# Conversion's shift through two PSUM banks, and a list scheduler with one time for the shared ports

## The chip, the cores and the metric

The kernel runs on one core of a Trainium2 chip. A core has engines that run their own queues of instructions in order: TensorE (PE) for matmuls, whose weight loads are shown apart as PEld; VectorE (DVE); ScalarE (ACT); GpSimd (POOL); and SyncE (SP), which here only issues DMAs. SBUF is the large on-chip memory, PSUM the small one of eight banks into which PE writes its results; DVE and ACT read and write both.

The metric is the device time in microseconds (us) of one execution; lower is better. The kernel before takes 739.78 us, the median of three runs (738.67 to 739.96).

## The reference

Two blocks follow one another. In the first, every one of 8 batches and 8 heads has 512 tokens and 32 state rows of width 64, and each side attends to the other. In the second, the 4352 rows that come out (8 batches of 512 + 32 rows, 512 wide) go through a hidden layer of 2048 with the gate h * cos(h).

```python
    scores = scale * np.matmul(x, state.transpose(0, 1, 3, 2))
    ...
    xread = np.matmul(a, state)
    ...
    sread = np.matmul(a2, x)
    return np.concatenate([xread, sread], axis=2).astype(np.float32)
    ...
    h = x @ w_in
    g = h * np.cos(h)
    return (g @ w_out).astype(np.float32)
```

`x` and `state` are float32. The weights `w_in` (512 x 2048) and `w_out` (2048 x 512) arrive as float64, so the kernel makes float32 of them itself.

## The kernel before

**Stages.** The batches are taken in four pairs. For a token row the attention output is a weighted mix of the 32 state rows of its head, so the kernel multiplies the state by `w_in` first ("products", `per_head`, L312, copied out at L462) and then multiplies the attention weights by that result (`hidden`, L488). What `hidden` makes for 128 hidden columns of one batch is called a tile; a batch has 16, the first pair 32 (steps 0 to 31, `FIRST = 32`). A tile passes through the gate: ACT rounds h to an integer (`gate`, L564), DVE takes the difference (`gate2`, L567), ACT the sine (`gate3`, L570), DVE the product with h (`gate4`, L584), which goes to `g_all`. In the first pair, `hidden` writes to two single PSUM banks in turn, so a tile's matmuls wait until `gate4` of the tile two before has read its bank. Output products with `w_out` are L640 for the first pair's first batch, and a seven-product form (L772) for everything after, for which sums of quarters of the weights (`inner`, L689; `sums_of`, L1325) are formed and kept in DRAM (`blocks_kept`).

**Conversion.** `fetch` (L210) brings a piece of float64 weights to SBUF as pairs of 32-bit words. `convert` makes float32 of it in five steps: "1" on ACT (L223) takes the absolute high word as a float with a changed exponent; "2" on ACT (L226) takes the top bits of the low word; "b" on DVE (L229) shifts the result of "1" left by 3, in place; "c" on DVE (L232) puts in the sign from the high word; "d" on POOL (L237) adds what "2" made. There are 18 pieces: 0 to 3 have 512 columns, 4 to 17 have 1024.

**The side banks.** Two PSUM banks, `h_pairs[1]` with the halves `side_banks`, are used in the first pair for the products L312 and for one set of state transposes (L161). The planner calls their halves `sd00`, `sd01`, `sd10`, `sd11`. The two remaining pairs of banks are `at` (attention) and `acc` (output products).

**The order.** Up to the end of the first pair, and a little into the next, the order of instructions comes from a list scheduler that runs while the program is built. `first_pair_tasks` lists tasks with an engine, an estimated cost, the names of what they read and write, a due step and a mark `shares`[...]. `link` turns due steps to times (22 + PACE * step) and finds what each task must wait for. `first_pair` takes, engine by engine, the task that can start soonest, and among those within NEAR of it the one due first; a task marked `shares` is put behind POOL's task of that time (`pool_busy`). Where PE would idle early on, dummy matmuls (`warm`, L952) are put in. The estimates only decide the order; on the chip every engine follows its queue, and semaphores hold it where a result is missing. After the first pair a hand-written plan sets the order (`later_pair`, `plan`, `stages`), which the change doesn't touch.

Of the kernel before, what the change touches and what calls it, by code (L numbers as in the profile page):

```python
# [11 lines left out]
I32 = mybir.dt.int32  # L12
# [10 lines left out]
def kernel(  # L23
# [189 lines left out]
    def convert(i, p):  # L213
# [7 lines left out]
        e = e.bitcast(I32)  # L221
        if p == "1":
            nc.scalar.activation(dst, raw.bitcast(F32)[:, :, :, 1],  # L223
                                 func=ACTF.Abs, scale=2.0 ** -112)
        elif p == "2":
            nc.scalar.activation(e, raw.bitcast(U32)[:, :, :, 0],  # L226
                                 func=ACTF.Copy, scale=2.0 ** -29)
        elif p == "b":
            nc.vector.tensor_scalar(bits, bits, 3, None,  # L229
                                    op0=ALU.logical_shift_left)  # L230
        elif p == "c":
            nc.vector.scalar_tensor_tensor(out=bits, in0=raw[:, :, :, 1],  # L232
                                           scalar=-2 ** 31, in1=bits,
                                           op0=ALU.bitwise_and,
                                           op1=ALU.bitwise_xor)
        else:
            nc.gpsimd.tensor_tensor(bits, bits, e, op=ALU.add)  # L237
# [10 lines left out]
    class Attention:  # L248
# [207 lines left out]
        def products_kept(self, nt, bank=None, c0=0, c1=WC, copy=None,  # L456
                          js=(0, 1)):
            to = at if bank is None else side_banks
            if c0 == 0:
                sw_of[self.b, nt] = sw_all[:, nt % 2]  # L460
# [257 lines left out]
    class Product:  # L718
# [4 lines left out]
        def __init__(self, name, pr, row):  # L723
# [5 lines left out]
            products.append(self)  # L729
            self.first = len(stage_list)  # L730
# [392 lines left out]
    def first_pair_tasks():  # L1123
# [35 lines left out]
        def conversion(i, due):  # L1159
            n = 512 if i < 4 else 1024  # L1160
            raw, w, e = raw_of(i), weight_of(i), low_of(i)
            if i > (6 if f64 else 4):
                add("sp", .4, lambda: fetch(i), "", raw, due - 3)
            for p, engine, cost, r, wr, sh in (
                    ("1", "act", act(n) + .05, raw, w, False),
                    ("2", "act", act(n) + .05, raw, e, False),
                    ("b", "dve", n * .0007 + .03, w, w, True),
                    ("c", "dve", dve(n), raw + " " + w, w, True),
# [4 lines left out]
        def attention(b, k):  # L1173
# [30 lines left out]
            m2 = k + 6 if b == 0 else k + 5  # L1204
            if b == 0:
# [3 lines left out]
                add("dve", .46, a.inverse1, "m10 m11", "m10 m11", k + 5)  # L1209
# [9 lines left out]
            if b == 0:  # L1219
# [4 lines left out]
                add("dve", .3, a.inverse2, "i20 i21", "i20 i21", m2 + 2)  # L1224
            else:
                add("act", 5.0, a.exps, "at0 at1 m20 m21",
                    f"z{z}0 z{z}1 xT2 xT3 i20 i21 m20 m21", m2)
                for j in range(2):
# [3 lines left out]
                    "m10 m11 i20 i21", k + 7)  # L1232
# [54 lines left out]
        def tile_(t, k):  # L1287
# [11 lines left out]
                k + 2)  # L1299
# [97 lines left out]
        def p5_tasks(k):  # L1397
# [3 lines left out]
            for i, (r, w) in enumerate(((lo, q1), (hi + " " + q1, q1),  # L1401
                                        (lo + " " + hi, q3)), 1):
                add("pool", 4 * pool(512), lambda i=i: pd.sums(i), r, w,
# [3 lines left out]
            for i in range(5):  # L1407
# [12 lines left out]
                elif i == 2:  # L1420
                    add("dve", .36, follow, "acc0 sums1", "sums2", at_)
                    add("pool", 4 * pool(512), lambda: pd.sums(4),
# [6 lines left out]
        def p3_sums(k):  # L1429
            pd = products_[1]  # L1430
            add("pool", 4 * pool(512), lambda: pd.sums(1),
# [17 lines left out]
        for step, what in (  # L1449
                (1, lambda: attention_late(0, 1)),  # L1450
                (3, lambda: products(0, 1, 3)),
                (3, lambda: add("pe", .4, lambda: states(1, side_banks[0]),
                                "held0", "sd00 sd01", 6)),
                (3, lambda: add("act", .53,
                                lambda: states_kept(1, side_banks[0]),
                                "sd00 sd01", "stT1", 6)),
                (5, lambda: attention(1, 5.0)),
                (7, lambda: products(0, 2, 7)),
                (11, lambda: products(0, 3, 11)),
                (13, lambda: products(1, 0, 15)),  # L1460
                (13, lambda: attention_late(1, 14)),
                (13, lambda: inner(0, a11, 5, temps[0], names(TEMPS), 15)),
                (15, lambda: sends(2, a22, 8, 17)),
                (15, lambda: sums_of(SQ, A21, A22, add_, 16, "pool")),
                (16, lambda: products(1, 1, 19)),
                (16, lambda: inner(3, matrix(SQ), SQ, temps[1], E, 15)),
                (17, lambda: sums_of(A22, SQ, A11, sub_, 18, "pool")),
                (17, lambda: attention(2, 18)),
                (18, lambda: sums_of(A21, A11, A21, sub_, 19, "dve")),
                (20, lambda: products(1, 2, 23)),  # L1470
                (20, lambda: inner(5, matrix(A21), A21, temps[0],
                                   names(TEMPS), 20)),
                (20, lambda: sends(1, a12, 6, 22)),
                (21, lambda: inner(4, matrix(A22), A22, temps[1], E, 21)),
                (23, lambda: sums_of(SQ, A12, A22, sub_, 24, "dve")),
                (24, lambda: inner(6, matrix(SQ), SQ, temps[0], names(TEMPS),
                                   25)),
                (24, lambda: products(1, 3, 27)),
                (25, lambda: attention_late(2, 23.0)),
# [4 lines left out]
        for step, what in (  # L1484
                (26, lambda: outer(0, 2, 0, 0, 26, "dve")),
                (27, lambda: outer(0, 2, 0, 1, 27, "dve")),
                (28, lambda: tokens_of_next(30)),
                (28, lambda: products(2, 0, 28)),
                (28, lambda: p5_tasks(29.5)),
                (29, lambda: weight_columns(t32, 30)),  # L1490
                (29, lambda: add("dve", .7, lambda: halves(2, 0), "z00 z01",
                                 "E0", 30)),
                (29, lambda: add("dve", .7, lambda: halves(2, 1),
                                 "z00 z01 E0", "E1", 30)),
# [5 lines left out]
        for step, t in enumerate(all_tiles[0:FIRST]):  # L1500
# [3 lines left out]
            if 4 <= step < 4 + NH:  # L1504
                first(step - 4, step + 1)
            for i in range(NH):
                if SECOND_AT[i] == step:
                    second(i, step + 2)
# [6 lines left out]
    CONV_DUE = (3, 4.5, 3.5, 6, 7.5, 7, 9, 9.5, 10.5, 11, 12, 14.5, 14, 15)  # L1515
    PACE, NEAR, SEND = 3.8, 0.3, 2.5
# [37 lines left out]
    def first_pair():  # L1554
# [20 lines left out]
        pool_busy, cold = (0.0, 0.0), True  # L1575
        log = []
        while can:
            best = None
            for e in free:
# [4 lines left out]
                for t in mine:  # L1584
                    at_ = max(free[e], ready[t])
                    if t.shares and pool_busy[0] <= at_ < pool_busy[1]:
                        at_ = pool_busy[1]
                    starts[t] = at_
# [3 lines left out]
                if best is None or starts[t] < best[0]:  # L1592
                    best = starts[t], t
            at_, t = best
# [11 lines left out]
            if t.engine == "pool":  # L1606
                pool_busy = at_, end
# [139 lines left out]
```

## Time and profile before

| what | value |
|---|---|
| median of 3 runs | 739.78 us (738.67 to 739.96) |
| the profiled execution | 740.65 us, of which the span from first to last instruction is 738.9 |
| PE busy | 708.2 us, 96% of the span |
| DVE, ACT, POOL busy | 506.8, 347.3, 542.5 us |
| mean granted PE clock | 0.993 of full speed |
| DMA | 111.33 MB, mean 151 GB/s |

The busy shares in 40 slices of 18.5 us each (a digit is a tenth, 9 is 90% or more) show that the first six slices, about the first pair, differ from the rest:

```profile
PE   8898889999999999999999999999999999999997
DVE  4989979957866668849756577768665467355550
ACT  5799675654463446343634464344634533211110
POOL 1557789375998997588998665879989665799600
```

PE has digits of 8 only there, while DVE and ACT are at their fullest. In the page's groups of instructions, a row gives line, engine, operation, output and input, count, busy time and mean duration; a group's mean mixes free and delayed executions, so single ones are read from the timeline.

### The profile page before, as it was taken

The page shows a single profiled execution, that of the slowest core. Times are in us where ns is not written, and L with a number is a line of the kernel's source. Part 1 is how long each engine was busy: PE and PEld are TensorE (multiplying, and loading weights), DVE is VectorE, ACT ScalarE, POOL GpSimd, SP SyncE. Part 2 cuts the span into 40 slices and gives each one's busy share as a digit, 9 for nine tenths or more (in the row PEclk, how much of TensorE's full clock was granted, in tenths as well). Part 3 has the DMA queues.
Part 4 walks back from the last instruction along what each step waited for, and adds up shares of the span by engine and source line. Part 5 has one row for each costly group of instructions (what it writes and reads, how often), then busy time and mean ns, then how long its engine had stood idle before and what let it go on. Part 6 is the DMA issues. An engine that isn't in the chain of part 4 may idle for free.

```text
span 738.9 us, 10734 instructions
## 1 busy us (share of the span) xinstructions
PE 708.2 (96%) x3626; PEld 519.0 (70%) x3626; DVE 506.8 (69%) x703; ACT 347.3 (47%) x586; POOL 542.5 (73%) x524
## 2 busy tenths in 40 slices
PE   8898889999999999999999999999999999999997
PEld 3343343477778878777778788777688788888886
DVE  4989979957866668849756577768665467355550
ACT  5799675654463446343634464344634533211110
POOL 1557789375998997588998665879989665799600
PEclk9999999999999999999999999999999999999999
DMA  9966799536346964693238635762225466456662
GB/s 297 285 192 193 236 265 301 122 96 150 87 128 117 214 172 115 142 197 86 82 80 168 160 96 116 147 154 83 75 68 119 115 205 143 108 156 203 155 152 46
DMA packets 204021, 111.33 MB, mean 151 GB/s; under 512 B 149888, under 2 KB 166784, under 8 KB 203968
## 3 DMA queue, kind: packets, MB, share of 16 engines
q1 hardware_dynamic: 202880, 110.14, 57.4%
q8 instruction: 29, 0.48, 0.3%
q10 hardware_dynamic: 960, 0.39, 0.2%
q14 instruction: 24, 0.20, 0.1%
q0 software_dynamic: 128, 0.13, 0.1%
HBM read 87.03 MB, written 23.59 MB: 150 GB/s over the span
## 4 chain that ended last, share of the span: by engine, by line
PE 59%; POOL 21%; DVE 9%; issue 3%; DMA 3%; ACT 2%; SPq 1%; ACTq 0%; POOLq 0%; DVEq 0%
PE o L772 29%; POOL g_all L715 16%; PE h L543 13%; PE h L488 8%; POOL swS_all L521 3%; PE at L312 3%; PE at L877 2%; DMA held<-in_state_dram 2%; PE o L640 2%; POOL sw_all L521 2%; DVE g_all L715 1%; PE at L417 1%; DVE q_all L567 1%; DVE g_all L232 1%; DVE g_all L584 1%
## 5 line engine op out<-in xcount | busy, mean ns | idle before, releaser
L715 POOL TENSOR_TENSOR g_all<-g_all 128x512 f32<-128x512 f32 x252 | 332.5, 1349 | 61.8 <-DVE g_all L715 40.4
L772 PE MATMUL o<-g_all 128*128 128x256 f32 x1456 | 343.7, 381 | 2.4 <-POOL g_all L715 2.4
L772 PEld LDWEIGHTS o<-g_all 128*128 128x128 f32 x1456 | 273.7, 190 | 49.7 <-issue 5.7
L567 DVE TENSOR_TENSOR q_all<-q_all,h 128x1024 f32<-128x1024 int32 (+1 forms) x88 | 85.3, 971 | 40.7 <-ACT q_all L564 40.4
L564 ACT ACTIVATE q_all<-h 128x1024 int32<-128x1024 f32 (+1 forms) x88 | 73.1, 833 | 81.2 <-PE h L543 35.1
L584 DVE TENSOR_TENSOR g_all<-h,q_all 128x1024 f32<-128x1024 f32 (+1 forms) x88 | 85.7, 973 | 24.5 <-ACT q_all L570 23.6
L570 ACT ACTIVATE q_all<-q_all,halfpi 128x1024 f32<-128x1024 f32 (+1 forms) x88 | 84.2, 957 | 38.7 <-DVE q_all L567 38.5
L551 DVE TENSOR_TENSOR h<-h,sums_all 128x256 f32<-128x256 f32 x96 | 41.3, 430 | 77.5 <-PE h L543 60.2
L488 PE MATMUL h<-aT_all,sw_all 128*128 128x512 f32 x128 | 64.0, 628 | 13.0 <-DVE g_all L584 12.3
L543 PE MATMUL h<-aT_all,sw_all 128*128 128x256 f32 x192 | 59.6, 392 | 3.8 <-DVE g_all L584 3.4
L543 PE MATMUL h<-aS_all,swS_all 128*128 128x256 f32 x192 | 60.2, 395 | 2.6 <-ACT sums_all L529 1.8
L715 DVE TENSOR_TENSOR g_all<-g_all 128x1024 f32<-128x1024 f32 x42 | 62.0, 1490 | 0.1
L543 PE MATMUL h<-aS_all,sw_all 128*128 128x256 f32 x192 | 58.0, 384 | 0.1
L488 PEld LDWEIGHTS h<-aT_all,sw_all 128*128 128x128 f32 x128 | 23.2, 195 | 44.3 <-issue 21.5
L521 POOL TENSOR_TENSOR swS_all<-sw_all 128x128 f32<-128x128 f32 x48 | 22.5, 468 | 41.8 <-ACT sw_all L462 41.8
L543 PEld LDWEIGHTS h<-aS_all,swS_all 128*128 128x128 f32 x192 | 33.9, 189 | 27.0 <-issue 12.1
L780 ACT COPY o<-o 128x256 f32<-128x256 f32 x26 | 9.3, 357 | 85.1 <-PE o L772 85.1
L543 PEld LDWEIGHTS h<-aT_all,sw_all 128*128 128x128 f32 x192 | 34.5, 189 | 16.3 <-DVE g_all L584 12.2
L237 POOL TENSOR_TENSOR w_in<-w_in,aS_all 128x1024 int32<-128x1024 int32 (+1 forms) x10 | 22.3, 2241 | 29.9 <-DVE w_in L232 27.2
L787 ACT COPY o<-sums_all 128x256 f32<-128x256 f32 x26 | 9.8, 378 | 68.2 <-PE o L772 68.2
L543 PEld LDWEIGHTS h<-aS_all,sw_all 128*128 128x128 f32 x192 | 35.6, 190 | 8.2 <-DVE h L551 2.7
L607 DVE SCALAR_TENSOR_TENSOR held<-o,held 128x512 f32<-128x512 f32 x38 | 25.9, 681 | 13.7 <-PE o L772 13.1
(116 smaller groups left out, 931.6 us busy)
## 6 DMA issues: line engine op xcount, KB each, us to landing
g_all<-blocks_kept SPq DMA_DIRECT2D x206, 256.0 KB, 2.8
blocks_kept<-g_all SPq DMA_DIRECT2D x48, 256.0 KB, 3.9
g_all<-in_moe_w_out_dram SPq DMA_DIRECT2D x8, 1024.0 KB, 5.7
out_dram<-ot SPq DMA_DIRECT2D x128, 64.0 KB, 2.0
g_all<-in_moe_w_in_dram SPq DMA_DIRECT2D x6, 1024.0 KB, 7.1
x_b<-in_x_dram SPq DMA_DIRECT2D x24, 256.0 KB, 4.7
xT<-in_x_dram SPq DMA_DIRECT2D x80, 64.0 KB, 2.8
x_b<-in_x_dram SPq DMA_DIRECT2D x16, 128.0 KB, 4.3
```

Of the source, the lines that this page charges most:

```text
L237: nc.gpsimd.tensor_tensor(bits, bits, e, op=ALU.add)
L488: nc.tensor.matmul(out=t.hp, lhsT=t.lhs(i), rhs=t.rhs(i), start=(i == 0), stop=(i == t.kn - 1))
L521: nc.gpsimd.tensor_tensor(o, x1, x2, op=op)
L543: nc.tensor.matmul(out=out_, lhsT=w, rhs=r, start=start, stop=True, skip_group_check=True)
L551: nc.vector.tensor_tensor(o, h2[:, LO], sums_all[:, 0], op=ALU.add)
L564: nc.scalar.activation(t.q.bitcast(I32), t.hp, func=ACTF.Copy, bias=0.25)
L567: nc.vector.tensor_tensor(t.q, t.q.bitcast(I32), t.hp, op=ALU.subtract)
L570: nc.scalar.activation(t.q, t.q, func=ACTF.Sin, bias=halfpi, scale=-TWO_PI)
L584: nc.vector.tensor_tensor(g, t.hp, t.q, op=ALU.mult)
L607: nc.vector.scalar_tensor_tensor(out=out.t[:, ch], in0=bank, scalar=TWO_PI, in1=b.t[:, ch], op0=ALU.mult, op1=ALU.add)
L715: engine.tensor_tensor(o[:, i:i + n], x1[:, i:i + n], x2[:, i:i + n], op=ALU.subtract)
L772: nc.tensor.matmul(out=o, lhsT=ring[(self.first + k) % NB][:, i], rhs=g[:, i], start=(start and i == 0), stop=(i == QT - 1), skip_group_ch ...
```

## The change

Four things are changed, all of them before the end of the first pair.

- In `convert`, step "b" of the pieces of 1024 columns (4 to 17) writes its shifted words to the two side banks in PSUM (`shifted`), and step "c" reads them there and writes the weights' tile as before. Pieces 0 to 3 stay in SBUF.
- The planner's tasks follow: for those pieces "b" and "c" are no longer marked `shares`, "b" has the cost of a DVE operation at the normal rate, and both name the side banks. Some small DVE tasks (the inverses, `halves`) are newly marked `shares`, and the cost of POOL's sums for the seven-product form is halved in the plan.
- The scheduler keeps one time, `lock`[...]; POOL's tasks wait for it too, and of tasks with the same start the one that asked first goes first.
- Nearly all due steps, and PACE and NEAR, have new values. `products_kept` sets up its entry of `sw_of` at whichever half comes first, so the halves of the first columns can come in either order.

```diff
@@ convert
+        shifted = bits if i < 4 else h_pairs[1].bitcast(I32)
...
         elif p == "b":
-            nc.vector.tensor_scalar(bits, bits, 3, None,
+            nc.vector.tensor_scalar(shifted, bits, 3, None,
                                     op0=ALU.logical_shift_left)
         elif p == "c":
             nc.vector.scalar_tensor_tensor(out=bits, in0=raw[:, :, :, 1],
-                                           scalar=-2 ** 31, in1=bits,
+                                           scalar=-2 ** 31, in1=shifted,
@@ products_kept
-            if c0 == 0:
+            if (self.b, nt) not in sw_of:
@@ conversion
+            x, narrow = (w, True) if i < 4 else ("sd00 sd01 sd10 sd11", False)
+            b_cost = n * .0007 + .03 if narrow else dve(n)
...
-                    ("b", "dve", n * .0007 + .03, w, w, True),
-                    ("c", "dve", dve(n), raw + " " + w, w, True),
+                    ("b", "dve", b_cost, w, x, narrow),
+                    ("c", "dve", dve(n), raw + " " + x, w, narrow),
@@ attention
-                add("dve", .46, a.inverse1, "m10 m11", "m10 m11", k + 5)
+                add("dve", .46, a.inverse1, "m10 m11", "m10 m11", k + 5,
+                    True)
@@ first_pair_tasks, some of the due steps
-                (7, lambda: products(0, 2, 7)),
-                (11, lambda: products(0, 3, 11)),
-                (13, lambda: products(1, 0, 15)),
+                (7, lambda: products(0, 2, 8.5)),
+                (11, lambda: products(0, 3, 19.5)),
+                (13, lambda: products(1, 0, 21.5)),
...
-                (17, lambda: attention(2, 18)),
+                (17, lambda: attention(2, 23.5)),
...
-                first(step - 4, step + 1)
+                first(step - 4, step - 0.5)
...
-                    second(i, step + 2)
+                    second(i, step + 10.0)
...
-    CONV_DUE = (3, 4.5, 3.5, 6, 7.5, 7, 9, 9.5, 10.5, 11, 12, 14.5, 14, 15)
-    PACE, NEAR, SEND = 3.8, 0.3, 2.5
+    CONV_DUE = (1.9, 1.9, 3.0, 5.1, 5.3, 5.4, 9.4, 10.5, 10.6, 11.7, 12.2, 13.3, 13.0, 15.2)
+    PACE, NEAR, SEND = 3.6, 0.1, 2.5
@@ first_pair
-                    at_ = max(free[e], ready[t])
-                    if t.shares and pool_busy[0] <= at_ < pool_busy[1]:
-                        at_ = pool_busy[1]
-                    starts[t] = at_
+                    asked = max(free[e], ready[t])
+                    shares = t.shares or e == "pool"
+                    starts[t] = max(asked, lock) if shares else asked
...
-                if best is None or starts[t] < best[0]:
-                    best = starts[t], t
+                asked = max(free[e], ready[t])
+                if best is None or (starts[t], asked) < best[0:2]:
+                    best = starts[t], asked, t
...
-            if t.engine == "pool":
-                pool_busy = at_, end
+            if t.shares or t.engine == "pool":
+                lock = end
```

## The prediction

> **What bounds the kernel now.** I first cut the span into stretches. Columns: stretch and length, then the busy time of PE, PEld, DVE, ACT and POOL with instruction counts, the granted clock, the DMA share, GB/s.
>
> ```profile
> core 0: us, PE busy (x) PEld busy (x) DVE busy (x) ACT busy (x) POOL busy (x), PEclk, DMA share, GB/s
> 20.00:36.00 16.00, 13.23 (x90) 6.35 (x91) 15.79 (x28) 12.36 (x20) 7.12 (x5) 1.00 0.92 279
> 36.00:100.50 64.50, 54.75 (x246) 22.81 (x245) 59.31 (x69) 55.49 (x84) 45.91 (x22) 0.95 0.73 210
> 100.50:145.00 44.50, 42.57 (x188) 19.75 (x187) 39.34 (x50) 28.00 (x54) 35.87 (x24) 1.00 0.79 236
> 145.00:172.00 27.00, 27.00 (x126) 17.81 (x126) 14.77 (x21) 13.74 (x26) 16.16 (x20) 1.00 0.45 103
> 172.00:738.90 566.90, 554.12 (x2925) 444.62 (x2923) 367.99 (x520) 227.80 (x392) 432.43 (x444) 1.00 0.53 130
> ```
>
> From 145 us on PE is the bound, and no edit reaches past the first pair of batches, which ends near 172. What can change lies between 20 and 145: there PE is idle 2.77 + 9.75 + 1.93 = 14.4 us, while DVE is busy 59.3 of 64.5 us in the long stretch. The waits of PE up to 185 us (engine, line and what it waited for; us in total, times, longest) name the cause:
>
> ```profile
> PE h L488 <- DVE g_all L584: 12.3, 9, 3.5
> PE h L488 <- DVE aT_all L393: 0.7, 1, 0.7
> ```
>
> A tile's matmuls wait for a bank that the last gate step (L584) of the tile two before frees, and that step is late in DVE's queue. Why DVE is late shows in its timeline (start, duration, line, operation):
>
> ```profile
> 70.84 2.03 DVE L373 TENSOR_SCALAR i_all<-i_all 128x34 f32<-128x34 f32 x1
> 74.33 0.69 DVE L229 TENSOR_SCALAR g_all<-g_all 128x1024 int32<-128x1024 int32 x1
> 75.05 1.23 DVE L232 SCALAR_TENSOR_TENSOR g_all<-g_all 128x1024 int32<-128x1024 int32 x1
> 80.31 1.76 DVE L229 TENSOR_SCALAR g_all<-g_all 128x1024 int32<-128x1024 int32 x1
> 83.19 3.40 DVE L232 SCALAR_TENSOR_TENSOR g_all<-g_all 128x1024 int32<-128x1024 int32 x1
> 83.17 2.34 POOL L237 TENSOR_TENSOR g_all<-g_all,aS_all 128x1024 int32<-128x1024 int32 x1
> 166.07 1.22 DVE L567 TENSOR_TENSOR q_all<-q_all,h 128x1024 f32<-128x1024 int32 x1 [1.05 <-ACT q_all L564]
> ```
>
> The same shift takes 0.69 or 1.76, the same combination 1.23 or 3.40; the long one began with POOL's L237. That is a lock between DVE and POOL. Finally PE's clock after a pause (timeline, then a stretch as above):
>
> ```profile
> 82.73 2.90 PE L488 MATMUL h<-aT_all,sw_all 128*128 128x512 f32 x4 [2.02 <-DVE g_all L584]
> 97.27 3.68 PE L488 MATMUL h<-aT_all,sw_all 128*128 128x512 f32 x4 [3.48 <-DVE g_all L584]
> 97.20:99.00 1.80, 1.73 (x2) 0.84 (x3) 1.80 (x3) 1.77 (x4) 1.72 (x2) 0.53 1.21 255
> ```
>
> **The change, part by part.** Part 1, the shift writes PSUM and the combination reads it there: the 14 conversions of 1024 columns (the four of 512 stay). Lock time that goes, as duration less the free one (0.69 a shift, 1.28 a pair, 1.22 a combination): shifts at 60.18 0.46, 64.71 1.60, 80.31 1.07, 92.12 1.07, 98.64 1.06; combinations at 83.19 2.18 and 100.43 0.95. Sum 8.4 us. What it costs: no row has a shift into PSUM. Lower end 0.60 (today's pace: two take 1.28 to 1.29); upper end 1.22, the L567 row of 1024 columns with a PSUM operand, whose pace, start to start, is 1.14. I take 1.14, since one PSUM operand is what the new shift has: 14 x (1.14 - 0.60) = 7.6 us. [...]the move alone hardly relieves DVE. It relieves POOL, which the same lock held: L1325 79.20 x2 took 4.00 for 2 x 1.27, 89.50 x2 3.83, L237 63.22 x2 6.03 for 2 x 2.36, and so on, about 8 us by the same subtraction. POOL bounds nothing before 145 (45.9 of 64.5), so I cost that at nothing; its cover is that slack.
>
> The combination stays at 1.14 (pace of L232 today). [...]The trace's L567 rows, one PSUM operand, agree: 0.67 to 0.71 throughout, also under POOL's work.
>
> A wait is added: both side banks now carry shifts, the weight products (L312) and the second state transposes. Behind a waiting shift queue the gate steps. Bounds: 0, or one product and its two copies, 1.02 + 1.07 us, for each of some four meetings, 8 us. In the new order each shift after a product has two or more DVE operations or attention's eight between; I take 0.
>
> Part 2, the new order, read from the order of the instructions in the changed program. The edits to costs, due steps, PACE, NEAR, the lock's time and the test on sw_of issue nothing themselves; they act through this order alone. (The weight sums L1325 stand at L1331 there, the other lines one or two further.) (a) Start. The second half of the first weight columns is converted first; all four shifts, four combinations, the two maxima and the two copies stand ahead of L373 and L393. Against today, where L393 ends at 23.8, there come 2 x 0.34 + 2 x 0.6 + 2 x 0.6 + 0.7 = 3.8 us before it, and POOL's d steps (4 x 1.27, from 18.6, each locking out a combination) reach to about 25. So the first tile starts near 28 instead of 23.35. Then, before the first L584: shift and combination three times (6.8), two gate steps, two state reads; first L584 at 37.3 for 33.5 today. One conversion more is then done. The third tile's L567 comes at about 40.6 (39.9 at best, 41.2 if PE runs at the lower clock after its pause around 24): 3.1 us later than 37.48.
> (b) From there to the L567 of the 17th tile, today 37.48 to 103.13 = 65.65 us. Today: 28 gate steps x 0.60 = 16.8; 12 shifts 7.2; 12 combinations x 1.13 = 13.6; attention 14 x 0.61 + 0.85 = 9.4; two L1325 2.3; sum 49.3. Lock: 8.4, L373 1.5, L393 1.0, L1325 0.8 = 11.7. Bracketed waits for ACT 3.5. Remainder 1.1. New: 16.8 + 11 shifts 12.5 + 11 combinations 12.5 + 9.4 + one L1325 1.1 = 52.3; lock only on L373, L393, L1325, which the planner now knows: 2.0 (ends 0 and 3); waits 3.5 + 1.0, because ACT has 13 us of work between the gates of the fifth and sixth tile (two table loads at 1.28 among it) and L584 of the sixth waits for it; remainder 1.1. Sum 59.9: 5.7 us less. With (a): 5.7 - 3.1 = 2.6 us earlier.
> (c) From the 17th tile on PE has the work. It is 0.8 us less (one second product, 1.72, done before; one L312 group, 1.02, and 0.1 later). The half clock at 97.27 goes if the 3.5 us pause goes: 3.68 - 1.84 = 1.8. Of the pauses after 100.5 (0.42, 1.16, 0.34) the 1.16 should go, since four second products (6.9 us) now stand beside the third attention: 0.9 net. One further warm-up matmul pair at the start fills a pause.
> (d) DMAs: the same transfers in another order. Two weight loads instead of one stand ahead of the eight x loads on SP's queue; [...]x then lands near 42, and its last use is near 46. Nothing on the path.
>
> Sum: 2.6 + 0.8 + 1.8 + 0.9 = **6.1 us less**. The profiled execution has 740.65 (span 738.9 and 1.75 around), so 734.55; it lies 0.87 above the median of the runs, which gives **733.7**.
>
> [...]here 2.02 us, shortly after pauses of 2.07 and 0.97, was enough for 0.74 and 0.58. [...]by the trace any 2 us pause can cost 1 to 2. The one I expect at the sixth tile (some 3 us) may so take back 1.8: in the range.
>
> **The rivals.**
> 1. *The start and the slow shifts win: slower.* For: the 7.6 us are sure and the first tile is 5 us late; the lock can move to L373, L393 and L1325, which stay. If (b) saves nothing, DVE is 3.1 us late; one more pause at half clock is 1.8; less 0.8 of work done: 4.1 us slower, 743.9. Decides from: L567 of the 17th tile after 105. Against: two thirds of the lock was on the operations moved.
> 2. *The combination still contends* (one of its inputs stays in SBUF): 2.18 + 0.95 stay, 736.8. Against: the L567 rows.
> 3. *Side banks:* one product's 2.1 us stalls twice: 733.7 + 4.2 = 737.9. For: a shift waits for PE and ACT together. Against: the distance in DVE's queue, above.
> 4. *PE stays fed:* ACT waits and lock both go (4.5 + 2.0), start only 2.4 late: 6 us more, 727.7. For: PE's idle time and slow clock (14.4, and about 3.5 of stretched tiles) allow it. Against: ACT is busy 55.5 of 64.5 us as well.
>
> **How the numbers follow.** Forecast, 730.5 to 736: 0.48. Rival 4, 724 to 730.5: 0.16. Rivals 2 and 3, 736 to 738.3: 0.18. Within 0.2% (738.3 to 741.3), about what can be told from no change: 0.08. Rival 1: 0.10. Faster 0.82. The range 727.5 to 739.0 leaves out rival 1, half of no change and the far end of 4, together just under 0.2; the forecast's own is 730.5 to 736.
>
> **What would show it.** L229 of 1024 columns into h near 1.2 each and never 1.7; its L232 never above 1.3; L237 at 2.34 to 2.4; first L488 near 28; L567 of the 17th tile near 100; no 3.68 us tile there; after it PE without pauses; after the first pair the same rows, earlier by one constant. A first L488 past 30, or the 17th tile past 105, would make it wrong; so would shifts at 0.7, to the other side.

## The result, and the profile after

The changed kernel takes 735.45 us in the median of five runs (733.81 to 736.73), the kernel before 739.78 (738.62 to 740.00). The ratio is 0.9944, 95% interval 0.9926 to 0.9962: 4.3 us faster. The profiled execution has 736.73 us, its span 734.9, where the kernel before had 740.65 and 738.9. The same kernel was run once more among the experiments (E12): 0.9943 (0.9923 to 0.9963), profiled at 735.53 with a span of 733.6.

In the changed file the lines stand one or two further: shift L230, combination L233, GpSimd's last step L238, `hidden` L489, gate L565, L568, L571, L585, output products L641 and L774, products L313 with their copies L463, first softmax L374 to L394, second softmax L357 and L362 with its transposes L401, weight sums L1331.

First the busy shares of the changed kernel in 40 slices of the span, from its page:

```profile
PE   8798899999999999999999999999999999999997
DVE  4889979868767567849756687768665367355551
ACT  4699975644544455443634373444634533211110
POOL 1557599557998896579989665879989665799600
```

PE falls from 8 to 7 in its second slice (18 to 37 us, the start), and rises from 8 to 9 in its sixth, the end of the long stretch. The same kernel in stretches (columns as in the prediction):

```profile
20.00:36.00 16.00, 11.08 (x55) 4.84 (x56) 14.09 (x20) 10.46 (x17) 7.04 (x5) 0.68 0.71 245
36.00:100.50 64.50, 59.82 (x288) 26.49 (x292) 59.52 (x78) 59.53 (x91) 42.70 (x24) 1.00 0.78 225
100.50:145.00 44.50, 44.50 (x216) 19.77 (x201) 37.27 (x51) 29.68 (x56) 34.32 (x29) 1.00 0.82 233
145.00:172.00 27.00, 26.47 (x121) 19.63 (x121) 16.74 (x24) 12.78 (x23) 14.39 (x15) 1.00 0.54 128
```

TensorE is idle 4.92 + 4.68 + 0 = 9.6 us between 20 and 145, 14.4 before. In the long stretch it gained 5.1 us of work although VectorE is as full as it was (59.5). The price stands in the first row: 2.2 us more idle time and a granted clock of 0.68. The waits of PE up to 185 us (us in total, times, longest):

```profile
PE h L489 <- DVE g_all L585: 4.3, 3, 2.6
PE at L401 <- ACT xT L362: 4.2, 1, 4.2
PE h L489 <- ACT sw_all L463: 0.5, 1, 0.5
```

The wait for the gate's last step fell from 12.3 to 4.3 us, and a new one of 4.24 us stands at the start. VectorE's timeline shows why the gate comes sooner, with one line of GpSimd's between:

```profile
31.07 1.22 DVE L233 SCALAR_TENSOR_TENSOR w_in<-g_all,h 128x1024 int32<-128x1024 int32 x1
32.33 1.23 DVE L230 TENSOR_SCALAR h<-w_in 128x1024 int32<-128x1024 int32 x1
33.59 1.22 DVE L233 SCALAR_TENSOR_TENSOR w_in<-g_all,h 128x1024 int32<-128x1024 int32 x1
32.44 4.90 POOL L238 TENSOR_TENSOR w_in<-w_in,aS_all 128x1024 int32<-128x1024 int32 x2 [7.55 <-DVE w_in L233]
79.89 0.18 DVE L374 TENSOR_SCALAR i_all<-i_all 128x34 f32<-128x34 f32 x1
92.92 1.98 DVE L1331 TENSOR_TENSOR g_all<-g_all 128x1024 f32<-128x1024 f32 x1
```

The combination at 33.59 runs wholly under GpSimd's L238 (32.44 to 37.34) and takes its free 1.22. All fourteen shifts of 1024 columns take 1.20 to 1.23 and all their combinations 1.21 to 1.23; the softmax step of 128x34 takes 0.18 for 2.03. Of the operations that had been locked between 36 and 105 us only a weight sum still takes longer than its free time (1.98 for 1.22).

### The profile page after: what moved, and what is told of

It is laid out like the page before. It is cut to its first block, busy times and chain, and to the rows that moved or that the text cites. A ratio compares the mean times of both kernels' runs of the same rounds, so it can differ in the third digit from the quotient of the medians.

```text
span 734.9 us, 10754 instructions
## 1 busy us (share of the span) xinstructions
PE 709.1 (96%) x3628; PEld 519.4 (71%) x3628; DVE 501.4 (68%) x703; ACT 347.0 (47%) x586; POOL 535.5 (73%) x524
## 4 chain that ended last, share of the span: by engine, by line
PE 64%; POOL 21%; DVE 7%; issue 3%; DMA 3%; ACT 2%; SPq 0%; ACTq 0%; DVEq 0%; POOLq 0%
PE o L774 29%; POOL g_all L716 16%; PE h L544 13%; PE h L489 10%; POOL swS_all L522 3%; PE at L313 3%; PE o L641 3%; PE at L879 2%; PE at L418 2%; POOL sw_all L522 2%; DMA g_all<-in_moe_w_in_dram 1%; DMA g_all<-blocks_kept 1%; DVE h L230 1%; PE o L879 1%; DVE w_in L233 1%
## 5 line engine op out<-in xcount | busy, mean ns | idle before, releaser
L774 PE MATMUL o<-g_all 128*128 128x256 f32 x1456 | 344.1, 381 | 2.9 <-POOL g_all L716 2.4
L774 PEld LDWEIGHTS o<-g_all 128*128 128x128 f32 x1456 | 273.6, 190 | 50.8 <-issue 5.0
L565 ACT ACTIVATE q_all<-h 128x1024 int32<-128x1024 f32 (+1 forms) x88 | 73.3, 833 | 86.8 <-PE h L544 37.8
L568 DVE TENSOR_TENSOR q_all<-q_all,h 128x1024 f32<-128x1024 int32 (+1 forms) x88 | 85.2, 969 | 40.2 <-ACT q_all L565 40.0
L585 DVE TENSOR_TENSOR g_all<-h,q_all 128x1024 f32<-128x1024 f32 (+1 forms) x88 | 85.6, 973 | 23.6 <-ACT q_all L571 22.7
L571 ACT ACTIVATE q_all<-q_all,halfpi 128x1024 f32<-128x1024 f32 (+1 forms) x88 | 84.0, 956 | 33.6 <-DVE q_all L568 33.3
L552 DVE TENSOR_TENSOR h<-h,sums_all 128x256 f32<-128x256 f32 x96 | 41.2, 429 | 76.6 <-PE h L544 59.4
L489 PE MATMUL h<-aT_all,sw_all 128*128 128x512 f32 x128 | 63.7, 627 | 4.8 <-DVE g_all L585 4.3
L716 DVE TENSOR_TENSOR g_all<-g_all 128x1024 f32<-128x1024 f32 x42 | 59.9, 1440 | 0.1
L489 PEld LDWEIGHTS h<-aT_all,sw_all 128*128 128x128 f32 x128 | 23.4, 197 | 36.7 <-issue 19.8
L544 PEld LDWEIGHTS h<-aT_all,sw_all 128*128 128x128 f32 x192 | 34.5, 189 | 16.3 <-DVE g_all L585 12.1
L238 POOL TENSOR_TENSOR w_in<-w_in,aS_all 128x1024 int32<-128x1024 int32 (+1 forms) x10 | 19.6, 1961 | 32.0 <-DVE w_in L233 31.9
```

Source lines behind the costliest of these rows:

```text
L489: nc.tensor.matmul(out=t.hp, lhsT=t.lhs(i), rhs=t.rhs(i), start=(i == 0), stop=(i == t.kn - 1))
L544: nc.tensor.matmul(out=out_, lhsT=w, rhs=r, start=start, stop=True, skip_group_check=True)
L552: nc.vector.tensor_tensor(o, h2[:, LO], sums_all[:, 0], op=ALU.add)
L565: nc.scalar.activation(t.q.bitcast(I32), t.hp, func=ACTF.Copy, bias=0.25)
L568: nc.vector.tensor_tensor(t.q, t.q.bitcast(I32), t.hp, op=ALU.subtract)
L571: nc.scalar.activation(t.q, t.q, func=ACTF.Sin, bias=halfpi, scale=-TWO_PI)
```

## The experiments

Each kernel's median and its ratio to the kernel before in the same set of runs (the kernel before had 739.78 in the changed kernel's own set; 739.42 in that of E1 to E4, 739.9 in that of E5 to E8, 739.5 in that of E9 to E11 and 740.62 in that of E12):

| kernel | place of the shift | order | us | ratio (95%) |
|---|---|---|---|---|
| changed | PSUM | new | 735.45 | 0.9944 (0.9926 to 0.9962) |
| E12, changed again | PSUM | new | 736.51 | 0.9943 (0.9923 to 0.9963) |
| E1 | PSUM | old | 745.1 | 1.0079 (1.0064 to 1.0094) |
| E2 | SBUF | new | 739.59 | 0.9997 (0.9988 to 1.0006) |
| E6 | PSUM | old planner, told of the banks | 746.14 | 1.0082 (1.0070 to 1.0095) |
| E7 | SBUF | new planner, told of SBUF | 747.49 | 1.0092 (1.0073 to 1.0110) |
| E8 | PSUM | new planner, all due steps old | 742.67 | 1.0038 (1.0026 to 1.0050) |
| E9 | PSUM | new, conversion's due steps old | 740.02 | 1.0008 (1.0001 to 1.0014) |
| E10 | PSUM | new, `pool_busy` as before | 736.69 | 0.9959 (0.9948 to 0.9971) |
| E3 | PSUM | new, 4 dummy matmuls | 734.74 | 0.9936 (0.9922 to 0.9950) |
| E4 | PSUM | new, exponentials first | 734.86 | 0.9932 (0.9915 to 0.9948) |
| E5 | PSUM | E4 and 2 dummy matmuls | 734.0 | 0.9914 (0.9901 to 0.9927) |
| E11 | PSUM | E5 and 2 more | 734.94 | 0.9938 (0.9921 to 0.9955) |

### Place and order apart: E1 and E2

E1 is the kernel before with the place alone, E2 the changed kernel without it:

```diff
E1, in the kernel before
+        shifted = bits if i < 4 else h_pairs[1].bitcast(I32)
-            nc.vector.tensor_scalar(bits, bits, 3, None,
+            nc.vector.tensor_scalar(shifted, bits, 3, None,
-                                           scalar=-2 ** 31, in1=bits,
+                                           scalar=-2 ** 31, in1=shifted,
E2, in the changed kernel
-        shifted = bits if i < 4 else h_pairs[1].bitcast(I32)
+        shifted = bits
```

> The kernel before with only the place of the shift changed: pieces 4 to 17 write it to the two side banks, nothing in the planner or its due steps is touched. It computes the same output. Theory A (the lock is what costs in the first pair, and the new order only uses the freedom): the seven locked b and c of the kernel before, 8.4 us, go, but fourteen shifts at 1.23 instead of 0.60 cost 8.8, so VectorE gains nothing by itself: 739 to 741 us, no shift above 1.3. Theory B (the order and the due steps are the whole gain, the place of the shift counts for nothing): the same 740 us. Theory C (the side banks make new waits in an order that was not planned for them): 741.5 us or more, with waits of shifts for ScalarE's or TensorE's use of the side banks.

> The changed kernel with only the place of the shift put back: in place in SBUF, the order of every engine that of the changed kernel. It computes the same output. Theory A (the new order lives on shifts that do not stop behind GpSimd): several shifts take 1 to 2 us instead of 0.6, the tiles of the first pair fall behind, 738 to 741 us. Theory B (the order alone is the gain): shifts at 0.6 for most pieces give VectorE 5 us back, 733 to 735.5 us, not slower than the changed kernel.

Neither half is worth anything by itself: the place alone costs 5.7 us, and with the order alone the time is that of the kernel before (0.2 us less, inside its interval). E1 leaves out what E6 below adds, the planner's knowledge that the shift uses the side banks. Other users of these banks are then not kept apart from it, and its output is not the same, unlike what was expected; its instructions and their sizes are those of the kernel before, and E6 has nearly the same ratio. At 745.1 E1 lies in the range of theory C; where its waits are is told with E6. E2, inside the range of theory A, shows the lock itself, in the timelines of VectorE and GpSimd:

```profile
28.98 0.69 DVE L230 TENSOR_SCALAR w_in<-w_in 128x1024 int32<-128x1024 int32 x1
29.70 3.25 DVE L233 SCALAR_TENSOR_TENSOR w_in<-g_all,w_in 128x1024 int32<-128x1024 int32 x1
29.21 2.66 POOL L238 TENSOR_TENSOR w_in<-w_in,aS_all 128x1024 int32<-128x1024 int32 x1 [5.21 <-DVE w_in L233]
33.47 2.55 DVE L230 TENSOR_SCALAR g_all<-g_all 128x1024 int32<-128x1024 int32 x1
```

The shift that meets nothing takes 0.69 again. The combination at 29.70 meets GpSimd's L238, which ends at 31.87; 1.08 us after that the combination ends as well, so nearly all of its own work (1.23) was done only then. "Shared port" in the title and the expectations is my word for this lock: the runs show its times (3.25 for 1.23 in this row), not its cause. Over the fourteen pieces the shifts of E2 exceed 0.69 by 4.2 us and the combinations exceed 1.23 by 8.6, together 12.8, for 14 x (1.23 - 0.69) = 7.6 saved. From the third tile's L568 to the 17th's, E2 needs 60.62 us (41.40 to 102.02), the changed kernel 56.16 (43.17 to 99.33). Of the 4.5 us between them these rows explain 4.1: 2.3 of locked shifts, 6.6 of locked combinations and 1.2 of a weight sum (3.17 for 1.98), less 11 x 0.54 for the faster shifts. The new order meets more of the lock than the old one did (12.8 us for 8.4), so without the new place it gains nothing.

### The planner's share: E6 to E10

```diff
E6, as E1, and in the planner
+            x = w if i < 4 else "sd00 sd01 sd10 sd11"
-                    ("b", "dve", n * .0007 + .03, w, w, True),
-                    ("c", "dve", dve(n), raw + " " + w, w, True),
+                    ("b", "dve", n * .0007 + .03, w, x, True),
+                    ("c", "dve", dve(n), raw + " " + x, w, True),
E7, as E2, and in the planner
-            x, narrow = (w, True) if i < 4 else ("sd00 sd01 sd10 sd11", False)
+            x, narrow = w, True
E8, in the changed kernel: all due steps, PACE, NEAR of the kernel before; halves not marked
E9, in the changed kernel
-    CONV_DUE = (1.9, 1.9, 3.0, 5.1, 5.3, 5.4, 9.4, 10.5, 10.6, 11.7, 12.2, 13.3, 13.0, 15.2)
+    CONV_DUE = (3, 4.5, 3.5, 6, 7.5, 7, 9, 9.5, 10.5, 11, 12, 14.5, 14, 15)
E10, in the changed kernel: pool_busy in place of lock, equal starts as before
```

> The kernel before with the shift in the side banks and the planner told so by name, so that it keeps other users of these banks apart; its costs, its treatment of the port and its due steps stay as they were. Same output. E1, where the planner did not know of the banks, took 745.1. If E1's extra 5.7 us were waits for the banks that a planner can avoid: 738.5 to 741, no loss and no gain from the place alone. If the 0.63 us that each of 14 shifts takes longer stand on the path of an order that was not planned for them: 743 to 746 again. If the place alone were the gain: 735 to 737.

> The changed kernel with the shift in place in SBUF and its planner told so (cost 0.75 and 0.64-type shares of the port for every piece), so that the list scheduler with one time for the port and the new due steps choose an order for shifts that can be locked. Same output. E2, with the changed kernel's own order, took 739.59. If E2 was slow only because its order did not expect the locks (the scheduler and the dues being the gain): 734 to 736. If the locks cost whatever order is chosen, because GpSimd is busy for two thirds of this stretch: 737.5 to 740, with locked or late shifts of 5 us in sum or more.

> The changed kernel (side banks, one time for the port, GpSimd's sums at half the planned cost) with all due steps, the pace and the tolerance of the kernel before. Same output. If the due steps do the ordering that the gain needs: 739 to 742, the first tile at 27 to 28 as before and the tiles of 30 to 100 us as far apart as before. If the scheduler and the place bring the gain whatever the due steps are: 734 to 737.

> The changed kernel with only the fourteen due steps of the conversion's pieces put back to those of the kernel before. Same output. E8, with all due steps, the pace and the tolerance put back, took 742.67 against 735.45. If the earlier conversions (pieces 4 and 5 at step 1.9 instead of 3 and 4.5, later ones 0.5 to 2 steps earlier) carry the order: 739 to 743, with TensorE waiting for a combination ahead of a product (L313 on L233) for 3 us or more. If the steps of the attention, the gates and the sums carry it: 735 to 737.

> The changed kernel with the planner's old treatment of the shared port (a sharing VectorE task waits only for the GpSimd task placed last, and GpSimd never waits); side banks, due steps and costs those of the changed kernel. Same output. If the one time for the port is part of the gain: 737.5 to 740, with more locked operations between 36 and 105 us. If it counts for little[...]: 734.5 to 736.5.

E6 rules out that E1 was slow only for want of a planner that knows the banks: 746.1, at the upper edge of its second range. Its long stretch and its two longest waits of PE:

```profile
36.00:100.50 64.50, 53.52 (x229) 23.14 (x230) 54.41 (x70) 51.35 (x78) 38.98 (x21) 0.95 0.65 199
83.18 1.96 PE L313 MATMUL h<-w_in,st_all 64*32 64x512 f32 x16 [4.63 <-DVE g_all L233]
97.77 1.09 PE L313 MATMUL h<-w_in,st_all 64*32 64x512 f32 x16 [2.90 <-DVE g_all L233]
```

VectorE is less busy than before (54.4 for 59.3 us) and no shift or combination is locked, yet TensorE works less (53.5 for 54.8). What the product at 83.18 waited for shows in the timelines of VectorE and GpSimd:

```profile
66.14 4.88 POOL L238 TENSOR_TENSOR w_in<-w_in,aS_all 128x1024 int32<-128x1024 int32 x2 [1.26 <-ACT aT_all L353]
81.82 1.22 DVE L233 SCALAR_TENSOR_TENSOR g_all<-g_all,h 128x1024 int32<-128x1024 int32 x1
86.34 1.23 DVE L230 TENSOR_SCALAR h<-g_all 128x1024 int32<-128x1024 int32 x1 [2.10 <-ACT sw_all L463]
```

The combination at 81.82 makes a piece of `w_out` (in `g_all`), which a product with `w_in` does not read, and the last pieces of `w_in` had been ready since 71.02. But the combination reads the shifted words from the side banks (`h`), to which the product writes: it ends at 83.04, and the product starts 0.14 us later. So the product waited for the banks. Shifts wait there too, for the copies of a product (86.34, 2.10 us). In all, products wait 7.5 us for combinations in E6; in E1 they wait 3.1 us for shifts and combinations. The lists of PE's waits have none of this for the kernel before and for the changed kernel. That is what theory C of E1 named: new waits at the side banks, in an order that was not planned for them. How E6's loss divides among these waits, the longer shifts and a granted clock of 0.95 was not taken apart.

E8 (742.7) lies 0.7 us above the range that stood for the due steps, E9 (740.0) inside it. With the due steps of the conversion alone put back, E9 loses 4.7 us, the whole gain (1.0008 less 0.9944, of 740 us), and products wait for combinations again, 4.7 us in E9 and 3.0 in E8. The longest such wait of E9, from PE's timeline with a line of GpSimd's and one of VectorE's, and that of E8:

```profile
59.53 1.10 PE L313 MATMUL h<-w_in,st_all 64*32 64x512 f32 x16 [4.08 <-DVE g_all L233]
56.95 2.36 POOL L238 TENSOR_TENSOR w_in<-w_in,aS_all 128x1024 int32<-128x1024 int32 x1 [6.36 <-DVE w_in L233]
58.16 1.22 DVE L233 SCALAR_TENSOR_TENSOR g_all<-g_all,h 128x1024 int32<-128x1024 int32 x1
```

```profile
78.75 1.09 PE L313 MATMUL h<-w_in,st_all 64*32 64x512 f32 x16 [2.99 <-DVE g_all L233]
```

In E8 it is the banks alone (the last piece of `w_in` was ready at 66.98). In E9 the product's own piece of `w_in` is ready at 59.31 and the banks are free at 59.38, so both are late together. The due steps of the conversion thus set two things: when a piece is done, and when the side banks are taken.

E7, the new planner told of the old place, missed both expectations: 747.5. Its stretches:

```profile
36.00:100.50 64.50, 56.22 (x253) 24.18 (x252) 54.88 (x73) 56.19 (x87) 34.53 (x17) 0.95 0.68 198
145.00:172.00 27.00, 22.35 (x82) 14.99 (x82) 14.90 (x22) 10.90 (x20) 24.69 (x24) 1.00 0.55 172
```

Every shift and combination is marked `shares` there, and the planner sets such tasks and GpSimd's one behind the other. GpSimd does 34.5 us in the long stretch instead of 42.7, the rest comes in the last (24.7 for 14.4), and there TensorE is idle for 4.65 us (3.9 of it in waits for VectorE, 0.8 in one for GpSimd). Some shifts are locked all the same (1.83, 2.56 and 1.75 for 0.69). How much of the loss is each was not taken apart. E7's due steps are those that were set for the side banks; an order sought under the new planner for shifts in SBUF was not tried. E10 lies 1.1 us above the changed kernel, between its two expectations and with overlapping intervals: what the one time `lock` is worth stays open. The halved cost of GpSimd's sums and the other due steps were not tried alone.

### The start: E3, E4, E5, E11, and the changed kernel again

```diff
E3: four dummy matmuls ahead of the first turn (L401); E5: two
+                def turned(j=j):
+                    if b == 0 and j == 0:
+                        warm(4, acc[0])
+                    a.turn(j)
E4 and E5: step "1" of piece 6 issued behind the second softmax's exponentials
+                tasks[-1].later = (i, p) == (6, "1")
...
+            if t.later:
+                held_back.append(t)
E11: E5, and two dummy matmuls ahead of the first tile
+                if n == 0:
+                    warm(2, acc[0])
                 hidden(t)
```

> The changed kernel with four dummy 128x512 matmuls put into TensorE's 4.24 us pause ahead of the first transposes of the second softmax (the L401 group). Same output. If the pause is what halves the clock afterwards: the first eight L489 take 3.6 to 3.8 us instead of 6.15 and the eight transposes about 1.2 instead of 1.97, the third tile's L568 moves from 43.2 to about 41 to 42, and the whole ends 1 to 2 us earlier (733.5 to 734.5). If the start's delay is set by VectorE and ScalarE alone: the matmuls are shorter, the third tile's L568 stays within 0.3 us of 43.2, and the time stays within 0.5 us of the changed kernel's.

> The changed kernel with one ScalarE instruction issued later: the sixth piece's first step (L224, 1.14 us at 23.93, which waits for a DMA) behind the two exponentials of the second softmax instead of ahead of them; all else in its order. Same output. If this place in ScalarE's queue is what made the start 2.6 us later than forecast: the exponentials start near 23.0 instead of 25.19, the first L489 near 28.2 instead of 29.55, TensorE's pause falls from 4.24 to about 2.6 us, the third tile's L568 from 43.2 to about 41.9, and the time falls by 1 to 1.5 us, to 734 to 734.5. If the pieces of the conversion set the first tiles: the third tile's L568 stays at 43 and the time at 735.5.

> E4 (the exponentials of the second softmax ahead of the sixth piece's first step) with two dummy matmuls in what is left of TensorE's pause. Same output. E3 and E4 took 734.74 and 734.86 in the median, with runs from 732.2 to 736.1. If the delayed exponentials and the half clock at the start are two costs that add: 733 to 734.3, the first L489 at 27 to 27.5 and 3.7 long, the third tile's L568 at 40 to 41. If the next wait behind them (the first softmax's L394 on VectorE, which the first L489 waited for in E4) takes it all: 734.5 to 735.5.

> E5 with two more dummy matmuls in TensorE's 2.10 us pause ahead of the very first L489, so that no pause of over 1 us is left before 60 us. Same output. In E5 (734.0) these eight L489 took 5.38 at half clock, in E4, after the same 2.10 us pause, 3.70. If the half clock at the start decides the spread: 732.5 to 733.7, the eight L489 at 3.7, the third tile's L568 at 39 to 40. If VectorE's conversions set the third tile anyway: 733.7 to 734.5, L568 still at 40.

> The changed kernel once more, nothing altered: its first profile has the sixth piece's transfer at 23.93, the first eight L489 at half clock (6.15) and the third tile's L568 at 43.17, and E3 to E5 and E11, which mend the start, have it at 39.9 to 40.7 but end only 0.5 to 1.5 us earlier in the median. If the late start belongs to the kernel: again an L568 at 42.5 or later, and a median of 735.2 to 736. If it belonged to that one execution: L568 at 40.5 to 42, and a median of 734.5 to 735.2, so that the mended kernels gain nothing that lasts.

In the changed kernel's first profile ScalarE's queue and TensorE read so (ACT's timeline, then PE's):

```profile
23.93 1.14 ACT L224 ACTIVATE g_all<-g_all 128x1024 f32<-128x1024 f32 x1 [1.92 <-DMA g_all<-in_moe_w_out_dram]
25.19 0.69 ACT L362 ACTIVATE xT<-at,m_all 128x512 f32<-128x512 f32 x1
26.02 1.97 PE L401 MATMUL at<-ident,xT 128*128 128x128 f32 x8 [4.24 <-ACT xT L362]
29.55 6.15 PE L489 MATMUL h<-aT_all,sw_all 128*128 128x512 f32 x8 [0.53 <-ACT sw_all L463]
```

The exponential L362 had its input (the maxima, done at 22.84) but stood behind a conversion step that waited for its DMA; the eight matmuls after TensorE's pause then took 6.15 for 3.70. In the second execution (E12), the same lines:

```profile
22.53 1.13 ACT L224 ACTIVATE g_all<-g_all 128x1024 f32<-128x1024 f32 x1 [2.06 <-DMA g_all<-in_moe_w_out_dram]
24.61 1.33 PE L401 MATMUL at<-ident,xT 128*128 128x128 f32 x8 [3.51 <-ACT xT L362]
27.63 6.35 PE L489 MATMUL h<-aT_all,sw_all 128*128 128x512 f32 x8 [0.87 <-ACT sw_all L463]
```

The transfer came 1.4 us sooner, the third tile's L568 at 41.45 instead of 43.17, the granted clock low again (0.79 between 20 and 36 us, 0.68 in the first execution). E3, with L224 at 22.59, nearly E12's time, has the eight L489 at 3.70 and L568 at 40.51:

```profile
27.78 3.70 PE L489 MATMUL h<-aT_all,sw_all 128*128 128x512 f32 x8 [0.53 <-ACT sw_all L463]
```

The lower clock is worth 0.9 us there (41.45 less 40.51). E4 has L362 at 22.42 and L568 at 40.70, E5 at 40.03, E11 at 39.94. So the start can be 1 to 3 us earlier, and with the pause filled (E3) the granted clock between 20 and 36 us was 1.00. What the place of L224 in ScalarE's queue costs does not show as clearly: E4, which moves it, has the third tile no sooner than E3, which leaves it. Of the clock, E5 missed its expectation (5.38 for 3.7).

Little of this lasts. E5 ended inside its first range, E3 and E4 0.2 and 0.4 us above theirs, E11 (734.94) above both of its own. E12 has the third tile where its second expectation put it, but the ratio of the first run and a median (736.51) in neither range, so a late start in one profile says little about the median. The four kernels have ratios of 0.9914 to 0.9938, all below the changed kernel's 0.9944 and 0.9943, but every interval overlaps with both of its intervals. E5 is the fastest kernel that was run and surely faster than the kernel before; that it beats the changed kernel is likely and not settled. One reason shows in E4 and E5: the first L489 then waits 2.10 us for the first softmax on VectorE, and E11, which fills that pause too, starts its third tile only 0.1 us sooner than E5. A second is the side banks again: in E3, E4 and E11 a product waits 0.9 to 1.2 us for a combination of `w_out` near 36. A third is the clock, told at the end.

## Why the prediction was right, and where its sizes were off

The forecast was 733.7 us and faster; it came out at 735.45, inside the range and, by ratio, just outside the measured interval (733.7 / 739.78 = 0.9918). The direction and the mechanism were right: VectorE's lock and the order that it allows. That the sum came so near owes something to luck. Its parts missed by more than the whole, in opposite directions: in the first profiled execution (a) was 2.6 us worse than forecast, (b) 3.8 better, (c) 2.4 worse, and 0.9 was lost after the first pair, 2.1 together.

**Part 1, lock against slower shifts.** Shown. 8.4 us for 7.6 was called no relief by itself. The 1.14 of a shift behind the 7.6 was my estimate from the L567 row of 1024 columns, and that the combination would no longer wait was one from the L567 rows of 512 columns. In the changed kernel a shift takes VectorE 1.15 us from start to start on average (12.68 for 11 between the third and the 17th tile) for 1.14 forecast, a combination 1.20 (13.22 for 11) for 1.14, since a combination and a shift directly behind one another follow at 1.24 to 1.33. Both estimates held: the shift into PSUM takes 1.20 to 1.23 for 0.69 in SBUF, and the combination, with one input in SBUF and one in PSUM, takes its free 1.22 under GpSimd's work in the row at 33.59, and none of the fourteen takes more than 1.23. Waits for the side banks were taken as 0. In the new order that was nearly so: VectorE waited for a copy out of them once, 1.7 us in one execution and 0.5 in the other. In the old order it is not, and there the place alone makes the kernel 5.7 us slower (E1), which was not seen: the sum of part 1 was made on VectorE's busy time, while products on TensorE now stand behind the shifted words for 3.1 us (E1) and 7.5 (E6).

**Part 2 (a), the start: 3.1 us late forecast, 5.7 measured.** The first L489 came at 29.55 for 28, the third tile's L568 at 43.17 for 40.6. Two terms make up the 2.6 us: 1.7 separate that execution from E12, where piece 6's transfer came 1.4 us sooner. That the transfer is the cause fits the two traces; no run held it late alone. Its L224 stands in ScalarE's queue ahead of the exponentials, which the sum did not see, since it followed VectorE's queue alone and took the DMAs at nothing (term d, in which x at 42 was my estimate); 0.9 is the lower clock after the pause (the eight L489 at 6.35 in E12, 3.70 in E3), which I had left out of the forecast and kept as an end (41.2). Without both (E3) the tile comes at 40.5, as forecast.

**(b), to the 17th tile: 59.9 us forecast, 56.16 measured** (56.18 in E12). The gain is 9.5 us instead of 5.7. The ends of the stretch, in the kernel before and in the changed one, from VectorE's timeline:

```profile
37.48 0.69 DVE L567 TENSOR_TENSOR q_all<-q_all,h 128x512 f32<-128x512 int32 x1 [1.50 <-ACT q_all L564]
103.13 0.67 DVE L567 TENSOR_TENSOR q_all<-q_all,h 128x512 f32<-128x512 int32 x1
43.17 0.69 DVE L568 TENSOR_TENSOR q_all<-q_all,h 128x512 f32<-128x512 int32 x1
99.33 0.68 DVE L568 TENSOR_TENSOR q_all<-q_all,h 128x512 f32<-128x512 int32 x1
```

VectorE's time in the stretch, summed from start to start by line, against the terms: gate steps 17.1 for 16.8, shifts 12.7 for 12.5, combinations 13.2 for 12.5, attention 9.1 for 9.4; lock and L1331 together 1.9 for 3.1, since L374 and L394 are free now (0.18 for 2.03, and 1.27 for the two L394, 0.68 and 1.66 before); waits for ACT 2.2 for 4.5; nothing for the remainder of 1.1. The large miss is the waits for ScalarE: the block with two table loads (1.28 each) did hold tile eight's matmuls, by 2.55 us (at 66.06), but VectorE had conversions to do meanwhile, so that its own queue lost less.

**(c), TensorE after that: 3.5 us forecast, 1.1 measured** (none in E12). The pauses between 100.5 and 145 are gone as forecast (44.50 of 44.50), and so is the tile of 3.68 us at 97 (granted clock 0.54). But the 1.8 us that this gives was added to VectorE's lead at the 17th tile as if TensorE had the same lead. It had not (its tile there starts at 96.19 for 97.27), and the lower clock came back at the start: the eight L489 lose 2.45 us (granted clock 0.60) and the transposes 0.9 (0.50). Net, TensorE's lead at the end of the first pair is 4.9 us, about the idle time that it lost (14.4 - 9.6); in E12 it is 5.5 (165.73), what VectorE's lead was at the 17th tile. The same row of PE's timeline, before and after:

```profile
171.21 0.59 PE L543 MATMUL h<-aS_all,sw_all 128*128 128x256 f32 x2
166.33 0.59 PE L544 MATMUL h<-aS_all,sw_all 128*128 128x256 f32 x2
```

**After the first pair** the same rows should come earlier by one constant. In the first execution 0.9 of the lead was lost, 0.6 of it at one wait for a DMA, from PE's timeline:

```profile
250.29 1.99 PE L774 MATMUL o<-g_all 128*128 128x256 f32 x8 [0.59 <-DMA g_all<-blocks_kept]
```

E12 has no such wait and keeps 5.3 of 5.5. So the forecast of 6.1 from one execution to another met 3.9 in the first and 5.1 in the second (740.65 less 736.73 and 735.53), 4.3 in the medians.

**The rivals.** The start did lose what rival 1 said, and more, but (b) made it good. Rival 2 falls with the combinations at 1.22. Rival 3 was one wait of 0.5 to 1.7 us in the new order; in the old one waits at the banks are longer than it said (7.5 us of products in E6). Rival 4 had (b) right (ACT waits and lock both went), yet not the start.

## What to carry to other kernels

A place that frees an engine from a lock and an order that uses this may each be worth nothing or less than nothing alone (here 0.9997 with the order, 1.0079 with the place), so take them apart in both directions before crediting either. A bank that an operation borrows is one more thing that others wait for (7.5 us of products in E6), and an engine's busy time does not show it (VectorE in E6 54.4 us for 59.3): look in the waits of the bound engine. When such an operation gets slower but steadier (here 1.20 to 1.23 for 0.69 to 2.29 us), set the due times of what feeds the bound engine anew; here putting back those of the conversion alone took the whole gain away. In a sum for the start of a kernel, look at every engine's queue for an instruction that waits for a DMA ahead of the one you follow; here it seems to have cost 1.7 us in one execution and little in another.

## What the runs showed of the hardware that was not expected

**After pauses of 2.1 to 2.6 us TensorE ran its matmuls in 3.70 or 5.38 us, in 1.98 or 3.53.** The same program point, from PE's timeline, in E4 and in E5 (2.10 us pause before both; the granted clock between 20 and 36 us was 1.00 in the one and 0.89 in the other):

```profile
27.27 3.70 PE L489 MATMUL h<-aT_all,sw_all 128*128 128x512 f32 x8 [2.10 <-DVE i_all L374]
```

```profile
27.17 5.38 PE L489 MATMUL h<-aT_all,sw_all 128*128 128x512 f32 x8 [2.10 <-DVE i_all L374]
```

At the tile near 63 us it is the other way round: 2.56 us in E5 and 2.55 in the changed kernel left the four matmuls at 1.98, while after 2.39 in E4 they took 3.53 (granted clock between 36 and 100.5 us: 1.00 in E5 and the changed kernel, 0.97 in E4):

```profile
63.62 3.53 PE L489 MATMUL h<-aT_all,sw_all 128*128 128x512 f32 x4 [2.39 <-DVE g_all L585]
```

The length of the pause alone does not decide it, and no run shows what does. Of the 1 to 2 us that the prediction gave to any pause of 2 us, E5 lost 1.68 (5.38 less 3.70) and E4 nothing at that point. In E12 the runs fall in line with the mean clock: spans of 732.1 to 733.6 at a clock of 0.995, 734.4 at 0.993, 735.5 to 735.7 at 0.991. In the first five runs they do so less (733.5 at 0.992, 733.8 at 0.995), and three runs of E11 at 0.998 have 733.0, 733.1 and 736.1, so there is at least one more cause of some 3 us that no run here names.

**Dependent operations started 0.1 to 0.2 us later on VectorE.** In the changed kernel's first pair a combination that reads what the shift just ahead of it wrote starts 1.26 or 1.27 us after it (31.07 less 29.81), a shift that overwrites what the combination ahead has read 1.24 to 1.33 (32.33 less 31.07 is 1.26), while a gate step that does not depend on what stands ahead starts 1.11 to 1.14 after a shift or combination (99.33 less 98.20, 97.60 less 96.46).
